# Roots of batch 0 on ScalarE and VectorE, another order of the first loads, and a new plan in an attention and gated-unit kernel

## The chip, the core and the metric

The kernel runs on one core of one Trainium2 chip. The core has TensorE (PE, matrix products; PEld is its weight load), VectorE (DVE), ScalarE (ACT), GpSimd (POOL) and SyncE (SP), which here only issues DMAs. The metric is the device time of one execution in microseconds (us). Groups in the profile give busy time in us and the mean of one instruction in nanoseconds (ns).

## The reference

Eight batches, eight heads, 576 tokens, 64 values in a head; all in float32. The weights come as float64 and are narrowed on the chip.

```python
def _attn_ref(q, k, v, g_norm):
    kv = np.einsum('bhsd,bhse->bhde', k, v)
    out = np.einsum('bhsd,bhde->bhse', q, kv)
    rms = np.sqrt(np.mean(out * out, axis=-1, keepdims=True) + 1e-06)
    return (out / rms * g_norm).astype(np.float32)

def _moe_ref(x, w_val, conv_w, w_out):        # x: (8, 576, 512), the heads side by side
    ...
    for k in range(K):                         # K = 5, causal
        gate_pre += conv_w[k][None, None, :] * xp[:, k:k + S, :]
    gate = 1.0 / (1.0 + np.exp(-gate_pre))
    val = x @ w_val
    return (gate * val @ w_out).astype(np.float32)
```

## The kernel before

Each batch goes through one chain. Two sums of products, k against v for each head (`kv_product`), give a 64x64 matrix a head; `kv_copy` moves them into a block-diagonal tile. `turn_q_rows` and `sort_q` transpose q of batches 0 and 1 on PE (later batches: `turn_q` on DVE). `raw_product` multiplies q by the matrices in five chunks of tokens: chunk 4 (64 tokens) first, then 3, 2, 1, 0 (128 each). For each chunk ACT squares (`square`, L499), DVE sums over a head (`sums`, L507), POOL raises the sum to the power -0.5 (`powers`, L513), and the result scales the chunk (`normalise`; on DVE at L528 for batches 0 to 2). The scaled chunk is transposed (`turn_x` on PE, `keep_x` on ACT for batches 0 and 1) into xT. From xT come the gate (`gate_start`, four `gate_tap`s on DVE, `gate_end`, a sigmoid on ACT) and the value product (`val_product` L590 for batches 0 and 1; later batches use a form with seven products instead of eight, `val_fast` L640). `gated` multiplies both, and an output product follows (`out_product` L671, or `fast_product` L735), then copy and store.

The weights, conv_w as one piece (cw), w_val and w_out as four pieces each, are loaded as pairs of 32-bit words by `stage_weight` into a ring of three buffers (w64) and narrowed to float32 in eight steps of `narrow_weight`: three on ACT, five on DVE. A w64 buffer is free again when step 6 is done. q of a batch is loaded as its last 64 tokens and two halves of the heads (`load_q_rows`, batches 0 and 1), k and v as two halves each (`load_half`), and their last 64 tokens as `load_tails`. All these loads are issued by SP, in order.

The order of all work is made when the program is built. Each step is given to a planner with its engine, an estimated time, a due time ("want"), what it needs and gives, the ring buffers it takes and frees, and for a DMA the time of its transfer ("load"). The planner runs a list schedule: of the steps that can start, it takes the one that can start first, and among equals the one with the smallest want. A table SHIFTS adds an offset to the wants of single steps, by the function's name and the batch (or the piece of weight). A step can't start earlier than its want less "ahead", which is 40 us, and 0 for loads. The list gives the order in which each engine gets its instructions; the engines themselves then wait on semaphores, not on planned times. While PE has nothing before 60 us of planned time, `keep_warm` (L397) fills the gap with products of the identity that are not used.

The wants of the loads at the start:

```python
    weight(("cw", 0), 0.0, 0.1, 0.1)
    ...
    loads_q(0, 0.01)
    loads_kv(0, 0.04)
    attention(0, 18.0, 1.8, 10.0, 5.0)
    for jt in range(NK):
        weight(("wval", jt), 0.09 + 0.01 * jt, 16.0 + 3.0 * jt, 0.5)
    ...
    loads_q(1, 0.14)
    loads_kv(1, 0.2)
    ...
        weight(("wout", jt), 0.3 + 0.01 * jt, begin + 1.0 + 4.6 * jt, 0.57)
```

Of the kernel before, what the change touches and what calls it, by code (L numbers as in the profile page):

```python
# [15 lines left out]
P = 128  # L16
# [5 lines left out]
    "fast_product": {1: 26, 2: 2, 3: 6},  # L22
    "gate_end": {7: 1.5},
    "gate_start": {4: 18.5},
    "gate_tap": {1: 38.5, 2: 38.5, 3: 74, 4: 70, 5: 49.5, 6: 86.5, 7: 45},
    "halo": {4: -0.5},
    "kv_product": {7: -5},
    "load_half": {("k", 3): -5.5, ("k", 4): -4, ("k", 5): 3.5, ("k", 7): -1.5, ("v", 0): -1.5,
        ("v", 4): -12, ("v", 5): -28.5, ("v", 6): -7.5, ("v", 7): -1.5},
    "load_q": {2: 23.5, 5: 17.5, 6: 8, 7: -9},  # L30
    "load_q_rows": {0: -173.5},
    "load_tails": {4: 11, 5: -2, 6: -21.5, 7: -18},
    "move_blocks": {7: 13},
    "normalise": {1: -26, 6: -27.5},
    "out_product": {0: 26},
    "powers": {3: -102, 4: 2, 7: -42.5},
    "raw_product": {2: -2, 4: -36, 6: -21.5, 7: 4.5},
    "square": {5: -170},
    "stage_weight": {("cw", 0): -313.5, ("wout", 1): -35.5, ("wval", 1): -123.5, ("wval", 2): -80.5,
        ("wval", 3): -85},  # L40
    "sums": {4: 2.5},
    "turn_blocks": {2: -1, 4: 48.5, 5: 32},
    "val_fast": {2: -5.5, 7: 18.5},
    "val_keep": {4: -120.5},
    "val_product": {0: 43, 1: 29},
    "weight_sums": {1: -14, 3: 19.5},
# [88 lines left out]
def kernel(  # L135
# [55 lines left out]
    FAST_VAL = range(2, B)  # L191
    FAST_OUT = range(2, B)
    ACT_NORM = range(3, B)
# [11 lines left out]
    def ps(kind, shape, name):  # L205
        return psum.tile(shape, FP32, tag=kind, bufs=BANKS[kind], name=name)
# [3 lines left out]
        "kv": 1, "kvbd": 2, "qT": 2, "tp": 1, "raw": 2, "mm": 4, "sq": 2, "ss": 3, "rt": 3,  # L210
# [188 lines left out]

    def kv_product(b, hp):  # L400
# [109 lines left out]
    def powers(b, c):  # L510
        n = heads(c)
        rt = work.tile([P, H], FP32, tag="rt", bufs=3, name=f"rt{b}_{c}")
        nc.gpsimd.tensor_tensor(  # L513
            out=rt[:, 0:n], in0=st["ss", b, c][:, 0:n], in1=mhalf[:, 0:n], op=ALU.pow)
        st["rt", b, c] = rt
# [252 lines left out]
    RATE = 0.27  # L768

# [6 lines left out]
    def attention(b, first, step, kv_first, turn_first):  # L776
# [40 lines left out]
        for n, c in enumerate(ORDER):  # L817
# [17 lines left out]
            )  # L835
            plan.add(
# [273 lines left out]
    for jt in range(NK):  # L1110
        weight(("wval", jt), 0.09 + 0.01 * jt, 16.0 + 3.0 * jt, 0.5)
# [70 lines left out]
```

## Time and profile before

| | us |
|---|---|
| median of 14 runs | 333.06 |
| lowest and highest | 332.35, 334.37 |
| the profiled execution, device time | 333.06 |
| its span, first to last instruction | 331.3 |
| busy: PE | 319.4 (96%) |
| busy: PEld, DVE | 245.4, 268.9 |
| busy: ACT, POOL | 185.8, 134.8 |
| DMA: moved, mean rate | 55.37 MB, 167 GB/s |

The span is what the profile's engines show; 1.76 us of the device time lie around it. A busy PE may be busy with filler, so its share alone doesn't say how much of it is needed. The windows in the prediction give, for stretches of the span, the busy time of PE, PEld, DVE, ACT and POOL (number of instructions in brackets), the granted PE clock as a share, and the share and rate of DMA. A line of the order of time gives start, duration, engine, line, operation, what it writes and reads, and in square brackets how long the engine was idle ahead of it and what released it. PEclk is full throughout: the mean granted clock is 0.997.

### The profile page before, as it was taken

What the parts mean: (1) busy time and instruction counts of PE and PEld (TensorE: products, weight loads), DVE (VectorE), ACT (ScalarE), POOL (GpSimd) and SP (SyncE); (2) the same over time, 40 slices, a digit from 0 to 9 for tenths busy, and PEclk for the clock granted to TensorE, in tenths of its full rate; (3) what the DMA queues carried; (4) which work ended last, traced back from release to release, by engine and by line L of the source; (5) the groups of instructions that cost most, each with busy time, mean ns of one, the idle gap of its engine ahead of it and who ended that gap; (6) DMA issues with size and microseconds to landing.
All of it is one profiled execution on the core that took longest, in us unless ns stands there. A gap on an engine that the chain in (4) does not pass through costs nothing.

```text
span 331.3 us, 6416 instructions
## 1 busy us (share of the span) xinstructions
PE 319.4 (96%) x2193; PEld 245.4 (74%) x2193; DVE 268.9 (81%) x479; ACT 185.8 (56%) x497; POOL 134.8 (41%) x178
## 2 busy tenths in 40 slices
PE   4999999999999999999999999999999999999993
PEld 4998877878755757587778758787885888888752
DVE  3168689799999729999999999999896697999601
ACT  3556965874366667675347848763676543534220
POOL 3006325203347969802558247777223274000000
PEclk9999999999999999999999999999999999999998
DMA  6999897697866886782966899465201235211233
GB/s 203 306 233 356 227 332 204 152 269 208 262 178 180 219 243 174 159 232 69 305 165 164 194 276 273 116 148 130 65 2 32 63 64 123 72 32 34 63 79 79
DMA packets 46014, 55.37 MB, mean 167 GB/s; under 512 B 15754, under 2 KB 36254, under 8 KB 45982
## 3 DMA queue, kind: packets, MB, share of 16 engines
q1 hardware_dynamic: 42558, 48.41, 53.1%
q0 software_dynamic: 3072, 6.30, 8.4%
q8 instruction: 17, 0.28, 0.4%
q10 hardware_dynamic: 352, 0.26, 0.4%
q14 instruction: 15, 0.12, 0.1%
HBM read 39.21 MB, written 9.44 MB: 147 GB/s over the span
## 4 chain that ended last, share of the span: by engine, by line
PE 81%; DVE 8%; DMA 3%; ACT 2%; issue 2%; SPq 2%; POOL 1%; DVEq 0%; ACTq 0%; POOLq 0%
PE va L640 13%; PE a L735 10%; PE raw L485 10%; PE cb L735 9%; PE out L671 8%; PE val L590 8%; PE vc L640 6%; PE out L678 4%; PE kv L408 4%; DVE gate L578 4%; PE vb L640 3%; PE qTps L446 3%; DMA vl<-in_v_dram 2%; PE kv L397 2%; PE xTps L538 2%
## 5 line engine op out<-in xcount | busy, mean ns | idle before, releaser
L513 POOL TENSOR_TENSOR rt<-ss,mhalf 128x8 f32<-128x8 f32 (+1 forms) x40 | 67.6, 1696 | 113.3 <-DVE ss L507 113.2
L578 DVE SCALAR_TENSOR_TENSOR gate<-xT,cwT,gate 128x576 f32<-128x576 f32 x128 | 99.1, 812 | 0.1
L561 POOL DMA_DIRECT2D xT<-y x96 | 52.9, 557 | 20.8 <-PE vc L640 7.5
L524 ACT ACTIVATE x<-raw,rt 128x64 f32<-128x64 f32 x180 | 39.6, 342 | 7.6 <-POOL rt L513 7.6
L485 PEld LDWEIGHTS raw<-kvbd,qT 128*128 128x128 f32 (+1 forms) x320 | 35.4, 180 | 8.4 <-issue 4.7
L485 PE MATMUL raw<-kvbd,qT 128*128 128x128 f32 (+1 forms) x320 | 39.1, 280 | 0.9 <-DVE x L528 0.6
L507 DVE TENSOR_REDUCE ss<-sq 128x8 f32<-128x520 f32 (+1 forms) x40 | 25.3, 633 | 10.2 <-ACT sq L499 9.7
L590 PE MATMUL val<-xT,wval 128*128 128x288 f32 x128 | 33.2, 409 | 0.0
L499 ACT ACTIVATE sq<-raw 128x512 f32<-128x512 f32 (+1 forms) x40 | 22.5, 562 | 18.5 <-PE raw L485 18.1
L671 PE MATMUL out<-wout,gv 128*128 128x512 f32 x64 | 28.5, 595 | 0.0
L590 PEld LDWEIGHTS val<-xT,wval 128*128 128x128 f32 x128 | 23.5, 190 | 5.8
L640 PE MATMUL va<-xs,vsum 128*128 128x288 f32 x96 | 27.3, 407 | 0.0
L603 DVE TENSOR_TENSOR gv<-gv,gate 128x576 f32<-128x576 f32 x32 | 23.6, 749 | 4.1 <-ACT gate L585 1.8
L585 ACT ACTIVATE gate<-gate 128x576 f32<-128x576 f32 x32 | 21.5, 690 | 8.9 <-DVE gate L578 8.8
L572 ACT ACTIVATE gate<-xT,cwT 128x576 f32<-128x576 f32 x32 | 24.1, 778 | 1.6 <-DVE gv L603 1.1
L735 PE MATMUL a<-wsum,sums 128*128 128x256 f32 x96 | 24.8, 381 | 0.0
L408 PEld LDWEIGHTS kv<-v,k 128*64 128x64 f32 x512 | 17.6, 137 | 5.6 <-issue 4.6
L671 PEld LDWEIGHTS out<-wout,gv 128*128 128x128 f32 x64 | 11.8, 190 | 13.2 <-issue 12.4
L640 PEld LDWEIGHTS va<-xs,vsum 128*128 128x128 f32 x96 | 18.0, 190 | 4.7
L744 DVE TENSOR_TENSOR ot<-cb,ot 128x256 f32<-128x256 f32 x24 | 10.0, 419 | 13.8 <-ACT ot L748 9.5
L408 PE MATMUL kv<-v,k 128*64 128x64 f32 x512 | 20.6, 226 | 0.2 <-DMA vl<-in_v_dram 0.2
L553 DVE STREAM_TRANSPOSE y<-x 128x512 f32<-128x512 f32 x24 | 16.8, 702 | 4.2 <-ACT x L524 4.2
(109 smaller groups left out, 563.8 us busy)
## 6 DMA issues: line engine op xcount, KB each, us to landing
q<-in_q_dram SPq DMA_DIRECT2D x96, 140.0 KB, 4.1
out_dram<-ot SPq DMA_DIRECT2D x140, 64.0 KB, 1.7
v<-in_v_dram SPq DMA_DIRECT2D x16, 512.0 KB, 6.2
k<-in_k_dram SPq DMA_DIRECT2D x16, 512.0 KB, 7.0
xT<-y POOLq DMA_DIRECT2D x96, 64.0 KB, 2.7
q<-in_q_dram SPq DMA_DIRECT2D x4, 512.0 KB, 6.3
w_wval<-in_moe_w_val_dram SPq DMA_DIRECT2D x4, 512.0 KB, 7.5
w_wout<-in_moe_w_out_dram SPq DMA_DIRECT2D x4, 512.0 KB, 6.6
```

What stands on the lines that cost most here:

```text
L408: nc.tensor.matmul(kvp[r * D:(r + 1) * D, hp, :], st["k", b, half][:, h, j, :] if j < NJ else kl[:, 2 * hp + r, :], st["v", b, half][:, h, ...
L485: nc.tensor.matmul(raw[row * m:(row + 1) * m, col * P:(col + 1) * P], st["qT", b][:, hp, c * P:c * P + m], kv_bd[b % 2][:, hp, :], start=T ...
L507: nc.vector.reduce_sum(out=ss[:, 0:n], in_=st["sq", b, c][:, 0:n], axis=AX.X)
L513: nc.gpsimd.tensor_tensor(out=rt[:, 0:n], in0=st["ss", b, c][:, 0:n], in1=mhalf[:, 0:n], op=ALU.pow)
L524: nc.scalar.activation(out=x[:, cols], in_=st["raw", b, c][:, cols], func=AF.Copy, scale=st["rt", b, c][:, h:h + 1])
L561: nc.gpsimd.dma_start(out=xTs[b % 2][i * TB:(i + 1) * TB, :, first:first + P], in_=y[a * TB:(a + 1) * TB, i])
L572: nc.scalar.activation(out=gate[:], in_=xTs[b % 2][:, jt, HALO:SX], func=AF.Copy, scale=cwT[:, K - 1, jt:jt + 1])
L578: nc.vector.scalar_tensor_tensor(out=gate[:], in0=xTs[b % 2][:, jt, tap * TB:tap * TB + S], scalar=cwT[:, tap, jt:jt + 1], in1=gate[:], op ...
L590: nc.tensor.matmul(val[:], wval[:, kc, jt * P:(jt + 1) * P], xTs[b % 2][:, kc, HALO + n * SV:HALO + (n + 1) * SV], start=(kc == 0), stop=( ...
L640: nc.tensor.matmul(st[bank, "val", b, mj][:], weights_[:, k], tokens()[:, k], start=(n in (0, 1, 3) and k == 0), stop=(k == NK // 2 - 1), ...
L671: nc.tensor.matmul(po[:], gv[:, jt, first:first + P], wout[:, jt, :], start=(jt == 0), stop=(jt == NK - 1),)
L735: nc.tensor.matmul(st[bank, i, p], tokens()[:, k], weights_[:, k], start=(n < 2 and k == 0), stop=(k == NK // 2 - 1), skip_group_check=True)
```

## The change

`powers` gets a second form for the chunks in `ROOTED`: ACT takes the square root (a new step, `root`, with a ring of its own), and DVE makes the reciprocal root of it in four small operations, the last three a Newton step. Chunks 3, 1 and 0 of batch 0 use it; chunks 4 and 2 of batch 0 and all other batches stay on POOL. A function `warm_up` issues 32 small products on PE at the start. The planner's rates and wants for the first loads and for batch 0's attention differ, its estimate of a power on POOL is 1.7 for 1.82, and the table SHIFTS is another one throughout.

```diff
 SHIFTS = {
-    "gate_tap": {1: 38.5, 2: 38.5, 3: 74, 4: 70, 5: 49.5, 6: 86.5, 7: 45},
-    "load_q_rows": {0: -173.5},
-    "stage_weight": {("cw", 0): -313.5, ("wout", 1): -35.5, ("wval", 1): -123.5, ("wval", 2): -80.5,
-        ("wval", 3): -85},
-    "val_product": {0: 43, 1: 29},
...
+    "gate_tap": {1: 46.5, 2: 6.5, 3: 56, 4: 67, 5: 82, 6: 82, 7: 27.5},
+    "load_half": {("k", 4): -26.5, ("k", 5): -25.5, ("k", 6): -12, ("v", 0): 2.5, ("v", 1): 5.5,
+        ("v", 2): 19, ("v", 3): 9.5, ("v", 4): -4, ("v", 5): -8.5, ("v", 6): -8.5, ("v", 7): -2.5},
+    "narrow_weight": {("wout", 0): 1.5, ("wout", 1): 3, ("wout", 2): -1.5, ("wval", 2): -15.5,
+        ("wval", 3): -47},
+    "stage_weight": {("wout", 0): -106.5, ("wout", 3): 66.5, ("wval", 0): -45},
+    "val_product": {1: 21.5},
...
+    ROOTED = {(0, NJ - 1), (0, 1), (0, 0)}
...
+    def warm_up():
+        banks = [ps("raw", [P, C], f"warm{n}") for n in range(2)]
+        for m in range(C // D):
+            for n in range(2):
+                for u in range(2):
+                    rows, to = (slice(r * D, (r + 1) * D) for r in (u ^ n, u))
+                    nc.tensor.matmul(
+                        banks[n][to, m * D:(m + 1) * D], ident[rows, 0:D], ident[rows, D:P],
+                        start=True, stop=True)
...
     def powers(b, c):
         n = heads(c)
-        rt = work.tile([P, H], FP32, tag="rt", bufs=3, name=f"rt{b}_{c}")
-        nc.gpsimd.tensor_tensor(
-            out=rt[:, 0:n], in0=st["ss", b, c][:, 0:n], in1=mhalf[:, 0:n], op=ALU.pow)
-        st["rt", b, c] = rt
+        st["rt", b, c] = rt = work.tile([P, H], FP32, tag="rt", bufs=3, name=f"rt{b}_{c}")
+        ss, rt = st["ss", b, c][:, 0:n], rt[:, 0:n]
+        if (b, c) not in ROOTED:
+            nc.gpsimd.tensor_tensor(out=rt, in0=ss, in1=mhalf[:, 0:n], op=ALU.pow)
+            return
+
+        t = st["root", b, c][:, 0:n]
+        nc.vector.reciprocal(rt, t)
+        nc.vector.tensor_tensor(out=t, in0=ss, in1=rt, op=ALU.mult)
+        for r, op, one in ((-0.5, ALU.mult, t), (1.5, ALU.add, rt)):
+            nc.vector.scalar_tensor_tensor(out=one, in0=t, scalar=r, in1=rt, op0=op, op1=ALU.mult)
+
+    def root(b, c):
+        n = heads(c)
+        st["root", b, c] = t = work.tile([P, H], FP32, tag="root", bufs=2, name=f"root{b}_{c}")
+        nc.scalar.activation(out=t[:, 0:n], in_=st["ss", b, c][:, 0:n], func=AF.Sqrt)
...
     RATE = 0.27
+    OPEN = 0.34
...
-                    takes=[(f"{name}{i}", b)], load=0.52 / RATE, ahead=0.0,
+                    takes=[(f"{name}{i}", b)], load=0.52 / (OPEN if b < 2 else RATE), ahead=0.0,
...
-                    load=(0.52 if i < 2 else 0.2) / RATE, ahead=0.0,
+                    load=0.52 / OPEN if i < 2 else 0.8, ahead=0.0,
...
-            load=0.52 * small / RATE, ahead=0.0,
+            load=0.52 * small / OPEN, ahead=0.0,
...
-    attention(0, 18.0, 1.8, 10.0, 5.0)
+    attention(0, 10.0, 1.0, 4.0, 2.0)
     for jt in range(NK):
-        weight(("wval", jt), 0.09 + 0.01 * jt, 16.0 + 3.0 * jt, 0.5)
+        weight(("wval", jt), 0.09 + 0.01 * jt, 20.0 + 4.0 * jt, 0.5)
...
         set_up()
+        warm_up()
```

## The prediction

> **What bounds the kernel now.** I read the windows of busy time first, then the groups of TensorE (PE) in the head, then PE's and SP's order of time there, last the roots on GpSimd (POOL).
>
> Windows (core us, then each engine's busy us):
> ```profile
> 0.00:22.90 22.90, 18.73 (x199) 17.60 (x199) 9.33 (x35) 10.39 (x26) 2.68 (x10) 1.00 0.96 248
> 22.90:39.75 16.85, 16.40 (x237) 14.77 (x237) 11.67 (x20) 13.35 (x33) 8.41 (x9) 1.00 0.99 292
> 39.75:60.00 20.25, 19.70 (x206) 15.87 (x206) 18.85 (x30) 12.57 (x25) 7.67 (x8) 1.00 0.77 239
> 60.00:100.00 40.00, 40.00 (x262) 28.97 (x257) 37.39 (x69) 23.03 (x48) 12.56 (x9) 1.00 0.82 222
> 100.00:140.00 40.00, 40.00 (x240) 24.79 (x239) 32.01 (x53) 26.90 (x82) 33.22 (x47) 1.00 0.76 197
> 140.00:220.00 80.00, 78.75 (x533) 61.31 (x533) 76.89 (x138) 50.61 (x161) 40.31 (x54) 1.00 0.74 196
> 220.00:300.00 80.00, 79.94 (x419) 63.36 (x418) 69.57 (x115) 42.20 (x111) 29.93 (x44) 1.00 0.29 70
> 300.00:331.30 31.30, 25.89 (x113) 18.77 (x111) 13.19 (x24) 6.75 (x16) 0.00 (x0) 0.97 0.23 59
> ```
> The first busy figure is PE's, the third VectorE's (DVE). From 39.75 (first value product) to 300, PE is idle 0.55 + 0 + 0 + 1.25 + 0.06 = 1.86 us; in the end stage 5.41. PE bounds everything after the head, with DVE close behind it (96% in 140 to 220). The head looks full too, but is not:
> ```profile
> L397 PE MATMUL kv<-ident 128*128 128x128 f32 x96 | 14.7, 310 | 0.2 <-ACT kvbd L418 0.2
> L446 PE MATMUL qTps<-ident,q 128*64 128x128 f32 (+1 forms) x160 | 10.4, 290 | 4.2 <-DMA q<-in_q_dram 4.2
> ```
> L397 is filler that computes nothing. Not work, of the span: filler 14.7, idle in the head 4.62, idle later 1.86 + 5.41, together 26.6 us. The rest, 304.7, the change doesn't touch. Where the head waits:
> ```profile
> 14.42 5.18 PE L397 MATMUL kv<-ident 128*128 128x128 f32 x44
> ...
> 20.84 2.05 PE L397 MATMUL kv<-ident 128*128 128x128 f32 x16
> 23.07 0.69 PE L408 MATMUL kv<-v,k 128*64 128x64 f32 x16 [0.17 <-DMA vl<-in_v_dram]
> ```
> ```profile
> 3.17 1.06 SPq L310 DMA_DIRECT2D w_wval<-in_moe_w_val_dram  x2
> ...
> 11.45 1.33 SPq L310 DMA_DIRECT2D w_wval<-in_moe_w_val_dram  x1
> 12.82 1.42 SPq L259 DMA_DIRECT2D k<-in_k_dram  x1
> ```
> Three value weights are issued ahead of the last half of k. That half, issued at 12.82 with landings of 8.8 to 10.1 us for k, is there at about 22.9; the second half of the k-v product starts at 23.07. (The release is put down to a later tail; by these landings k fits.) After it the roots go one by one on POOL:
> ```profile
> 28.89 6.43 POOL L513 TENSOR_TENSOR rt<-ss,mhalf 128x8 f32<-128x8 f32 x4 [0.45 <-DVE ss L507]
> ```
>
> **What the Trainium skill says.** "DMA: Bandwidth & Descriptors", Why small descriptors are slow (HBM only): each packet has a fixed cost, so 256-byte ones lose. The trace agrees: while tails pass (256 B rows), 3 us moved 0.63 MB (15 to 18 us) against 1.06 MB (9 to 12). "ScalarE: Activation LUTs", What ACT_TABLE_LOAD costs: 1283 ns for a load; the trace's two loads take 1283. Its section Table sets puts sqrt and sigmoid in different sets and cheap functions in every set; "ScalarE activation tables: per-element evaluation and per-set limits", Table sets in the compiler and the runtime, says loads are placed for the longest run. So the load at the start can be the sqrt set and the second, before the first sigmoid (47.63 us), stays: no load is added. No trace here shows a Sqrt. "TensorE: Matmul & The Clock Gate", What's actually happening: PE is slow until it has worked for some microseconds. Here 16 small transposes take 1.12 us at 4.16 and 0.68 at 24.38.
>
> **The change, part by part.** SP's order is read from the wants: of the loads that can start, the planner takes the one with the smallest want plus shift, and the nine weight pieces share three w64 slots, each free again only when its piece is converted. Tried on the kernel before, wants of -313.5 (cw), -173.5 (q), -123.4 and -84.9 (wval 1, 3), then v (-1.46), k, give exactly the recorded order.
>
> *Loads.* After: wout 0 (0.3 - 106.5) and wval 0 (0.09 - 45) come first, then cw (0), q, k 0, tails, k 1 (0.04), v 0 and v 1 (0.04 + 2.5). The w64 ring is full, so wval 1 to 3 stand behind v. Bytes up to the last of k and v: before 0.02 + q 1.18 + 3 weights 1.57 + k, v 2.10 + tails 0.26 = 5.13 MB; after, with 2 weights, 4.61. So one weight is gained, not three. By before's pace, (5.13 - 0.06) / (22.9 - 3.0) = 0.255 MB/us, 0.52 MB is 2.0 us. The first 3 us moved only 0.06 MB behind small transfers; a 512 KB transfer in front can fill the start sooner: 0 to 0.8, I take 0.3. Last half at 20.7 instead of 23.07: -2.4. The two weights put q back by 1.05 MB, some 3 us (q's tail at about 7, the rest at 10); PE's transposes of q (4.6 us warm: 0.68 + 4 x 0.98) still fit before v 0 at about 19, so this is hidden by the wait for v, and would cost nothing until q is 4 us later still. The other loads of SP (wval 1 to 3, q, k, v of batch 1) follow; up to batch 1's last k and v both orders carry some 9.7 MB, so those land near 36 us as before, and batch 1's raw product (45.24, wanted near 41 then) doesn't wait.
>
> *Roots.* Removed: three POOL powers of 1.61 us (6.43 / 4). Added for each: a Sqrt of 128x8 on ScalarE (ACT), 0.19 by the skill's 186 ns + 0.833 ns an element, up to 0.28 with a pointer bias, plus 1.28 if a table load falls there; and four small DVE steps. Nearest rows: 128x1 at 0.13 to 0.15 us, 128x20 from PSUM at 0.24; "VectorE: DVE Perf Modes", The TRN2 errata, prices a tensor_tensor at (N + 151) / 0.96, 0.166 us. I take 0.16 each, 0.65 for four; bounds 0.5 to 0.9. DVE gains 3 x 0.65 = 1.95 us, POOL loses 4.8. The Sqrt waits for the sums: ACT's weight conversions (0.72 each) queue behind it, and for them DVE; the four steps wait for the Sqrt, and on DVE sums and normalisations queue behind. On the path: before, five sums and five x from 26.82 to 36.10 with POOL pacing. With roots DVE paces: 0.42 + 4 x 0.69 sums, 1.95, 0.41 + 4 x 0.69 x = 8.3 us, end at 35.1 on the same clock. That is -1.0 for the last x, if no conversion falls between; each piece of weight does 2.97 us of DVE (0.42 + 0.69 + 0.42 + 0.69 + 0.75), so it may also be +2.
>
> *Batch 0's chain first.* After 23.07 the head still holds 18 fillers, 2.9 us, and 0.45 idle: 3.3 us. In the new order batch 1's q transposes (3.9), k-v and turning fill it, if q of batch 1 (7.1 MB, about 28 us) is there: after k-v at 20.7 come 1.4 product, about 0.9 copy to the bank, 4.4 raw, 0.9 turning two chunks, which ends at 28.3. I leave 1.7 us of loss (0.9 copy, 0.8 waits for x): -1.6. Bounds -3 and +2.
>
> *Warm-up.* 32 small matmuls after the identity is ready at 1.3 us, before q: 1.4 to 2.2 us in idle time. It costs nothing, since PE is idle for 4.2 us there; were q to land before 3.5 us, it would hold q's transposes up by what is left of it, and even that lies inside the wait for v. It speeds work that waits for v anyway.
>
> *Replanned rest.* 1.86 us of PE idle after the head is all that a better order there could win; the end stage needs its drain (last product ends 326.34, then copy and store, 5 us). I take 0; bounds -1.5 and, by rival D, +8.
>
> Sum: -2.4 - 1.6 = -4.0, with the roots' -1.0 inside the 1.6 (without them the last turnings, at 37.89 and 38.87, keep their places). The work PE does before the first value product is then 1.4 us less (half of batch 1's k-v is later), which is not lost. The profiled execution took 333.06 around a span of 331.30; the median is 333.06 too. 333.06 - 4.0 = 329.0.
>
> **Rivals.**
> - *A, forecast, 0.55:* 329.0, own range 327 to 331.
> - *B, the loads don't do what they say, 0.12:* wout 0 and wval 0 in front take the gain, tails and batch 1's small rows slow the end of v, and it lands near 22.5. Left are 0.5 + 1.0: 331.5. For it: k's halves took 8.8 to 10.1 us from issue to landing here, and the slow small rows of the tails now pass with 1.57 MB of k and v still behind them. Against: the byte count.
> - *C, more, 0.05:* the start runs at 0.35 MB/us, v at 19, and half of the 1.86 goes: -4.1 - 2 - 0.9 = 326.
> - *S, nothing left, 0.08:* PE starts earlier, but batch 1's k and v or weights come no sooner, and the head's gain comes back as waits: within 0.2%.
> - *D, slower, 0.20:* DVE becomes the bound in 140 to 220. It is idle there 3.1 of 80 us, and 8 of 40 in the stage before. PE running 4 us ahead eats this; the new wants of gates, turnings and sums, once they push more than 4 + 3.1 us of DVE work beyond 140, make PE wait for x sums and gated products. At 11 us of such work the waits are 8: -4 + 8 = 337. For it: 96% busy. Against: the tap shifts sum to 402 before and 367.5 after, so gates aren't later on the whole; and DVE has 20.2 idle us before 60 to be used (60 - 9.33 - 11.67 - 18.85).
>
> **How the numbers follow.** Faster by over 0.2% (about what a measurement of this kernel can tell from no change): A, B, C, 0.72; within: 0.08; slower: D, 0.20. The range 326.0 to 336.0 holds A, B, S, most of C and somewhat less than half of D.
>
> **What would show it.** SP's first issue is wout; second half of k-v at 20 to 21.5; fillers at or under 11 us; two table loads; four root steps at 0.13 to 0.2 us; first value product near 33 to 36; PE idle after it under 2.5 us until the end stage. Wrong if k-v starts after 22.5, if a third table load stands in the chain, or if PE waits for DVE by more than 4 us in 100 to 300.

## The result, and the profile after

The changed kernel takes 337.35 us (median of 10 runs, 336.05 to 339.74) against 332.90 us before (median of 48); the ratio is 1.0138 with the interval [1.0119, 1.0156]. It is 4.4 us slower where the prediction said 4 us faster. The span of the profiled execution is 335.5 us (before 331.3). The ratios here and below are made from fast runs alone, so that one can lie under the ratio of the medians. The ten executions go with their granted clock: the two at a mean of 0.996 took 336.05 and 336.44 us, the two at 0.989 took 339.55 and 339.74; the profiled one has 0.992, and the kernel before was at 0.996 or more whenever it ran beside an experiment. So of the 4.4 us about 1 goes with the clock, and some 3.3 are lost without it (an estimate from these figures).

The same windows as before, of the changed kernel (core us, then busy us of PE, PEld, DVE, ACT, POOL, the clock, the DMA share and GB/s):
```profile
0.00:22.90 22.90, 14.03 (x221) 12.96 (x223) 8.39 (x34) 9.52 (x24) 2.61 (x10) 0.99 0.99 247
22.90:39.75 16.85, 16.85 (x258) 15.19 (x259) 8.56 (x24) 11.64 (x32) 3.66 (x6) 0.91 0.92 266
39.75:60.00 20.25, 19.36 (x101) 15.26 (x100) 18.76 (x32) 13.93 (x27) 6.33 (x3) 1.00 0.83 240
60.00:100.00 40.00, 37.09 (x328) 28.62 (x327) 38.85 (x71) 23.02 (x45) 18.97 (x16) 1.00 0.71 207
...
140.00:220.00 80.00, 78.77 (x523) 61.86 (x522) 74.19 (x131) 50.41 (x156) 43.68 (x57) 1.00 0.75 201
```
Two things differ. PE, which was busy 40.00 of 40 us between 60 and 100, is busy 37.09, and VectorE is at 38.85 of 40 there (37.39 before). And up to 22.9 us PE does 4.7 us less, and comes out of it at a lower clock (0.91 in the second row; it was 1.00).

PE's waits, by what ended them (us in total, times, longest), and the same groups of fillers:
```profile
PE qTps L465 <- DMA q<-in_q_dram: 5.3, 1, 5.3
PE xTps L569 <- DVE x L559: 2.6, 1, 2.6
PE kv L427 <- DMA q<-in_q_dram: 1.8, 1, 1.8
```
```profile
L405 PE MATMUL kv<-ident 128*128 128x128 f32 x42 | 7.0, 327 | 0.9 <-ACT kvbd L437 0.9
L415 PE MATMUL warm<-ident 64*64 64x64 f32 x64 | 2.0, 314 | 1.4 <-POOL ident masks.py:199 1.4
```
Fillers fell from 14.7 to 7.0 us (and 2.0 of warm-up), but idle time rose from 11.9 to 19.7 us, so nothing was won by having fewer of them.

Busy time hides where the loss is, because fillers count as busy and a matmul at half clock counts double. I therefore priced each useful matmul of PE (no filler, no warm-up) at its full-clock duration and compared how much of it the two kernels have done by the same time. Positive is ahead of the kernel before; the count is good to about 0.5 us.
```
by (us)        20    30    40    50    60    70    80   100   300
changed      -0.6  -1.3  +0.6  -0.7  +0.8  -1.0  -3.2  -3.3  -4.7
```
So: about 1 us behind when batch 0's chain begins, 2 us won in it, 4.0 lost between 60 and 80, another 1.5 up to 300.

**The head.** SP's issues in the order of time (start, duration, queue, line):
```profile
8.45 1.33 SPq L267 DMA_DIRECT2D k<-in_k_dram  x1
9.82 1.86 SPq L276 DMA_DIRECT2D kl<-in_k_dram  x1
11.73 1.17 SPq L276 DMA_DIRECT2D vl<-in_v_dram  x1
12.95 2.92 SPq L267 DMA_DIRECT2D v<-in_v_dram  x2
...
25.97 3.48 SPq L318 DMA_DIRECT2D w_wval<-in_moe_w_val_dram  x3
```
Batch 1's tails (9.82 and 11.73) pass ahead of v; value weights 1 to 3 come at 25.97, behind k and v of both batches. PE in the same stretch:
```profile
21.05 0.69 PE L427 MATMUL kv<-v,k 128*64 128x64 f32 x16 [1.85 <-DMA q<-in_q_dram]
...
22.78 1.12 PE L427 MATMUL kv<-v,k 128*64 128x64 f32 x16 [0.35 <-DMA v<-in_v_dram]
...
26.56 4.43 PE L504 MATMUL raw<-kvbd,qT 128*64 128x128 f32 x40
...
39.37 2.11 PE L621 MATMUL val<-xT,wval 128*128 128x288 f32 x8
```
In the kernel before, the raw product:
```profile
25.70 4.43 PE L485 MATMUL raw<-kvbd,qT 128*64 128x128 f32 x40
```
(The pause of 1.85 is put down to q. The product doesn't read q; the first half of v, which it reads, landed at 20.9.) The second half of k-v starts at 22.78 instead of 23.07; after two pauses it takes 1.12 us for what took 0.69, since the granted clock is at half from 22.6 to 26.1 us, and the raw product starts at 26.56, 0.9 us later than before. One execution says little here. The first loads stand in this order in eight of the profiled kernels, and in them the second half began between 22.31 and 24.89 us; in three with the order of before between 22.42 and 23.07. And the half clock is not in all of them: in two kernels of the experiments below with the same head (one with a value product moved at the wait, one with batch 1's chain put earlier) k-v ran at full clock, and the first value product began at 38.29 and 38.19 us, 1.5 us earlier than before (39.75). ScalarE meanwhile, in batch 0's chain:
```profile
29.23 0.60 ACT L518 ACTIVATE sq<-raw 128x512 f32<-128x512 f32 x1 [0.30 <-PE raw L504]
29.85 1.28 ACT L546 ACT_TABLE_LOAD   x1
31.14 0.21 ACT L546 ACTIVATE root<-ss 128x8 f32<-128x8 f32 x1
31.26 1.07 ACT L518 ACTIVATE sq<-raw 128x512 f32<-128x512 f32 x2
```
A third table load stands before the first root, and the squares of the two last chunks stand behind it.

**60 to 80 us.** The wait of 2.6 us is one turning, of batch 1's last chunk:
```profile
68.44 0.66 PE L504 MATMUL raw<-kvbd,qT 128*64 128x128 f32 x8
71.69 0.63 PE L569 MATMUL xTps<-ident,x 128*128 128x128 f32 x4 [2.59 <-DVE x L559]
```
In the kernel before, the same chunk:
```profile
58.04 1.16 PE L485 MATMUL raw<-kvbd,qT 128*128 128x128 f32 x8
...
62.78 4.05 PE L590 MATMUL val<-xT,wval 128*128 128x288 f32 x16
66.66 0.60 PE L538 MATMUL xTps<-ident,x 128*128 128x128 f32 x4
67.10 9.87 PE L590 MATMUL val<-xT,wval 128*128 128x288 f32 x40
```
The chunk's raw product started at 63.46 (before at 58.04, and its turning at 66.66 without a wait). The raw products of batch 1 begin earlier than before (43.7 against 45.24), but chunk 2 stands behind four value products of batch 0 and chunk 1 behind three more. By 60 us all value products of batch 0 are used up, and the order puts only one of batch 1's ahead of this turning.

The plan itself has this wait. By the planner's own times, which are there when the program is built, PE is free at 62.67 and the turning starts at 65.98, 3.3 us later; the plan of the kernel before has no wait there. The new plan pays for it with a shorter head: its first value product stands at 34.21 us, against 40.16 in the plan of the kernel before, and the whole ends at 332.0 against 335.6. On the chip the wait came (2.6 us), and the shorter head didn't (39.37 against 39.75).

### The profile page after: what moved, and what is told of

Read it like the earlier page. It is cut to its first block, busy times and chain, and to the rows that moved or that the text cites. A ratio compares the mean times of both kernels' runs of the same rounds, so it can differ in the third digit from the quotient of the medians.

```text
span 335.5 us, 6442 instructions
## 1 busy us (share of the span) xinstructions
PE 315.8 (94%) x2203; PEld 240.6 (72%) x2203; DVE 269.8 (80%) x491; ACT 186.9 (56%) x501; POOL 136.9 (41%) x175
## 4 chain that ended last, share of the span: by engine, by line
PE 62%; DVE 13%; DMA 9%; ACT 5%; issue 3%; SPq 3%; POOL 3%; DVEq 0%; ACTq 0%; POOLq 0%
PE va L671 10%; PE out L702 8%; PE a L766 8%; PE cb L766 8%; PE val L621 7%; PE raw L504 6%; PE vc L671 5%; DMA q<-in_q_dram 4%; PE kv L427 4%; DVE gate L609 4%; PE out L709 3%; DMA v<-in_v_dram 3%; PE vb L671 3%; SPq L276 2%; POOL rt L534 2%
## 5 line engine op out<-in xcount | busy, mean ns | idle before, releaser
L534 POOL TENSOR_TENSOR rt<-ss,mhalf 128x8 f32<-128x8 f32 (+1 forms) x37 | 68.4, 1850 | 111.6 <-DVE ss L526 111.3
L427 PE MATMUL kv<-v,k 128*64 128x64 f32 x512 | 21.4, 231 | 2.2 <-DMA q<-in_q_dram 1.8
L427 PEld LDWEIGHTS kv<-v,k 128*64 128x64 f32 x512 | 18.6, 143 | 6.6 <-issue 4.2
L702 PEld LDWEIGHTS out<-wout,gv 128*128 128x128 f32 x64 | 11.9, 190 | 13.5 <-issue 13.2
L766 PEld LDWEIGHTS a<-wsum,sums 128*128 128x128 f32 x96 | 17.8, 190 | 2.9 <-ACT ot L781 0.3
```

The costliest lines, as they stand in the source:

```text
L427: nc.tensor.matmul(kvp[r * D:(r + 1) * D, hp, :], st["k", b, half][:, h, j, :] if j < NJ else kl[:, 2 * hp + r, :], st["v", b, half][:, h, ...
L534: nc.gpsimd.tensor_tensor(out=rt, in0=ss, in1=mhalf[:, 0:n], op=ALU.pow)
L702: nc.tensor.matmul(po[:], gv[:, jt, first:first + P], wout[:, jt, :], start=(jt == 0), stop=(jt == NK - 1),)
L766: nc.tensor.matmul(st[bank, i, p], tokens()[:, k], weights_[:, k], start=(n < 2 and k == 0), stop=(k == NK // 2 - 1), skip_group_check=True)
```

## The experiments

Each ratio is against the kernel before, run in turn with it on the same chip. "Ahead" and "behind" are useful PE work as in the table above.

**Parts of the change in its own order.** Only the named step differs from the changed kernel. Value weights without their conversion (and the same in the kernel before, as the yardstick):
```diff
     def narrow(key, dst, n):
+        if key[0] == "wval" and key[1] > 0:
+            if n == 6:
+                w = staged[key]
+                nc.vector.tensor_copy(
+                    dst, w[:, :, 1].rearrange("p (m c) -> p m c", m=dst.shape[1]))
+            return
```


> The changed kernel with its order of work untouched; pieces 1 to 3 of w_val are not converted but copied once as raw words (0.42 us of VectorE in place of 2.97, nothing on ScalarE), so the values are left out of the computation. Theory 1 (the late conversions of the value weights fill VectorE from 36 to 52 us and push batch 1's chain back, so TensorE waits at 68 to 73): the 2.6 us wait goes to under 0.7 and the time falls from 337.4 to 333 to 334.5. Theory 2 (it is TensorE's new order, all value products of batch 0 ahead of batch 1's chain): the wait stays over 2 us, the time falls by under 1 us.

> The same omission in the kernel before, pieces 1 to 3 of w_val copied and not converted, order untouched. Theory 1: here these conversions lie in idle VectorE time of the first 30 us, so nothing but noise: 332.5 to 333.2. If any VectorE or ScalarE work that is left out makes the kernel faster by itself: 2 us or more faster, and theory 1 gets no support from the other run.

Measured: 338.48 us, ratio 1.0101 [1.0038, 1.0165], and 332.77, 0.9999 [0.9982, 1.0016]. The first time says little, since its four executions lie between 334.32 and 339.79 us; the trace says more. The wait of 2.6 us at the turning is unchanged, although VectorE has only 10.6 us of work from 39.75 to 60 instead of 18.8. The freed time lies idle: its queue waits for the gate's first step on ScalarE, which comes 3.8 us after the first value product (4.1 in the changed kernel). Late conversions alone don't make this wait.

The roots back on GpSimd:
```diff
-        if (b, c) not in ROOTED:
+        if True:
             nc.gpsimd.tensor_tensor(out=rt, in0=ss, in1=mhalf[:, 0:n], op=ALU.pow)
             return
```


> The changed kernel with its order untouched, all roots back on GpSimd (no Sqrt, so no third table load). Theory 3 (the table load of 1.28 us and the root steps cost as much as GpSimd's queue saved): within 0.6 us of 337.4. Rival (the roots are worth having): GpSimd's powers stand one behind another again, the last x of batch 0 comes 1 to 2 us later, 338 to 339. Rival (the table load is what slowed it): 335.5 to 336.5.

Measured: 337.19 us, 1.0136 [1.0115, 1.0157]; the changed kernel has 1.0138. At the end these runs show no difference. In the head they show one: without the roots PE waits 1.3 us for x, and from the start of batch 0's raw product to the first value product it is 14.29 us; with them 12.81 (14.05 in the kernel before). That the 1.5 us aren't seen at the end may lie with the clock: this execution had no half clock in the head (its raw product began at 24.95) and one behind the wait of 2.6 us.

v of batch 0 moved ahead of batch 1's tails on SP:
```diff
+        vs = [f for f in found if f[1]["fn"] is load_half and f[1]["args"][0] == "v" and f[1]["args"][2] == 0]
+        found = [f for f in found if f not in vs]
+        at = next(n for n, f in enumerate(found) if f[1]["fn"] is load_tails and f[1]["args"][0] == 1)
+        found[at:at] = vs
```


> The changed kernel with one thing moved on SyncE's queue: v of batch 0 is issued ahead of batch 1's tails. Theory 4 (my count failed since these tails, 0.26 MB in rows of 256 B, pass before v): the second half of the k-v product starts at 20.7 to 21.5 and not at 22.8; the head ends 1 to 2 us earlier. If the wait at 68 to 73 comes from VectorE alone, the gain is eaten there and the time stays within 1 us of 337.4; if the head decides, 335.5 to 336.4.

Measured: 336.42 us, 1.0106 [1.0080, 1.0131]. PE in this run:
```profile
19.86 0.69 PE L427 MATMUL kv<-v,k 128*64 128x64 f32 x16 [0.45 <-DMA v<-in_v_dram]
...
21.82 0.69 PE L427 MATMUL kv<-v,k 128*64 128x64 f32 x16 [0.58 <-DMA v<-in_v_dram]
```
Both halves come about 1 us earlier and at full clock. This is the load order that the prediction assumed, and it gives 21.82, not 20.7. In the three other kernels below with v first it came at 21.75, 21.93 and 20.96; so all four lie under the eight with the tails first (22.31 to 24.89). This run is 2.2 us ahead at 40 us and about 3 behind at 80; the wait of 2.6 us is still there.

**Single steps at the wait.** A value product of batch 1 put ahead of the late turning, and, in another kernel, the sums of chunks (1,1) and (1,0) put right behind their squares (and x(1,0) two steps earlier, not shown):
```diff
+        move(pick(val_product, 1, 1, 1), pick(turn_x, 1, 0))
+        move(pick(keep_val, 1, 1, 1), pick(keep_x, 1, 0))
```
```diff
+        for c in (1, 0):
+            move(pick(sums, 1, c), pick(square, 1, c), 1)
```


> The changed kernel with its order untouched but for one product: TensorE does the value product of batch 1, piece 1, second half (1.94 us; it needs only chunks 4 to 2) ahead of the turning of chunk 0 and not behind it. Theory 2 (the new order leaves TensorE nothing to do while batch 1's last chunk is scaled): the wait at 69 to 72 falls from 2.6 to 0.6 to 0.9 us and the time by 1.5 to 3 us, to 334.5 to 336. Rival (the wait is only where a lag from the head comes out, so it turns up elsewhere): another wait of about 2 us within 10 us of it, time within 0.7 of 337.3.

> The changed kernel with its order untouched but for VectorE's queue in batch 1: the sums of chunks 1 and 0 stand directly behind their squares, and the scaling of chunk 0 two steps earlier, ahead of two steps of the output weights and of gate taps. Theory 5 (chunk 0's own chain is late since its steps queue on VectorE behind other work: its square ends at 65.3 and its sum starts at 67.6): chunk 0's x starts at 68.5 to 69.5 and not at 70.9, the wait falls to under 1.2 us, time 335 to 336.3. Rival (GpSimd's power sets it): x no earlier than 70, no gain.

Measured: 336.44 us, 1.0103 [1.0060, 1.0146], and 337.14, 1.0117 [1.0081, 1.0153]. In the first the wait splits into 0.45, 0.61 and 1.03 us within the next products; its time lies between the two forecasts. In the second x(1,0) starts at 70.28 instead of 70.86 and the turning waits 0.71, but then the value product waits 2.25 us for the copy of that turned chunk: on ScalarE it stands behind a gate's last step, which waits for a tap on VectorE. One step moved is one wait moved.

**The loads replanned.** The output weight's early want taken away and everything planned anew:
```diff
-    "stage_weight": {("wout", 0): -106.5, ("wout", 3): 66.5, ("wval", 0): -45},
+    "stage_weight": {("wout", 3): 66.5, ("wval", 0): -45},
```


> The changed kernel, planned anew with one shift taken out: piece 0 of w_out isn't due first. Then w64's oldest buffer is free early, and the other three value weights are issued between 9 and 18 us and not at 26 to 29. If the late value weights mattered, 334 to 335.5; after the run with the conversions left out I rather expect that they don't: 336 to 338, with VectorE less than 17 us busy from 40 to 60. A new plan moves everything a little, so under 1 us says nothing.

Measured: 350.87 us, 1.0528 [1.0471, 1.0585]. The value weights do load early again, so the three slots of w64 are what holds them back in the changed kernel: a slot comes free in the order in which it was taken, and the first is the output weight's, converted after 17 us. But the new plan loses 5 us at 90 to 100 and 11 more after 180. By its planner's own times this plan ends at 348.3 us, where the changed kernel's ends at 332.0; so this loss, too, stood in the plan before any run. A plan made from one different want moves the time by 13 us: three times what the whole change cost.

**Batch 1's chain put earlier.** In the first try its sums, powers and normalising stand ahead of taps and conversions on all engines, and raw products (1,1) and (1,0) earlier on PE; then with v first as well, and in a third kernel, with v in its old place, without the conversions of value weights 1 to 3:
```diff
+        put(pick(gate_tap, 0, 2, 1), (powers, 1, 3), (normalise, 1, 3))
+        put(pick(val_product, 0, 2, 0), (turn_x, 1, 3), (raw_product, 1, 1))
...
+        put(pick(kv_product, 2, 0), (turn_x, 1, 2), (raw_product, 1, 0), (val_product, 0, 3, 0))
```


> The changed kernel's loads, roots and fillers; only the steps of batch 1's chain (sums, powers, normalise, squares, turnings and raw products of chunks 3, 2, 1, 0) stand earlier on all four engines, ahead of gate taps and value products of batch 0. Theory (place in the queues): the loss of the changed kernel between 60 and 80 us comes from the steps of this chain standing late in in-order queues, while all value products of batch 0 are used up before. Then the wait of 2.6 us for the normalised chunk (1,0) falls under 0.5, no other PE wait over 1 us comes in its place up to 80 us, useful PE work at 80 us is 0 to 1.5 us behind the kernel before instead of 3.2, and the time is 334 to 335.5. Rival (DVE is simply full from 60 to 100 us): what is put ahead pushes taps and conversions back, a wait for DVE or for what follows it comes again within 30 us, work at 100 us is still 3 or more behind, and the time is 336.5 to 338.

> As the one with the chain put earlier, and v of batch 0 ahead of batch 1's k and v tails on SP as well. If both parts add (2.6 for the chain, 1 for the load): 333 to 334.5, about the kernel before. If DVE is full from 60 to 100 us, the earlier start only waits there: 336 to 337.5.

> The changed kernel with both at once: value weight pieces 1 to 3 are only copied instead of converted (their values are left out; some 8 us of VectorE less between 40 and 60 us), and batch 1's chain stands earlier on all engines. Each alone moved nothing that shows. Theory (the loss of 3 to 4 us between 60 and 80 us is VectorE work that the changed load order pushed behind 40 us, met by a chain that stands behind it in the queues, so that only both together lift it): PE waits at chunk (1,0)'s turning and the value products behind it fall from 4 to under 1 us in sum, useful PE work at 80 us is 0 to 1 us behind the kernel before, time 333 to 335. Rival (something else than VectorE sets the pace of that chain, for instance the round trip over four engines itself): the waits stay over 2.5 us, work at 80 us is over 2 behind, time 336 to 338.

Measured: 336.47 us, 1.0114 [1.0088, 1.0140]; 336.21, 1.0119 [1.0076, 1.0163]; 336.59, 1.0141 [1.0106, 1.0176]. The one wait became three of 1.5, 1.2 and 1.2 us, the same in the third kernel, and the work at 80 us is 2 to 3 us behind in all. By their numbers the rivals hold, but the trace shows that the edit missed its aim: raw product (1,2) still started at 52.1 us, behind four value products, so the chain was not begun earlier. These three don't separate the theories.

Hence the chain spread between the value products, one chunk behind each, without and with v first, and last with the two places mended at which those waited:
```diff
+            "PE": val_(0, 0) + val_(1, 1) + one_(turn_x, 4) + one_(raw_product, 2) + val_(1, 0) + one_(turn_x, 3)
+                + one_(raw_product, 1) + val_(2, 1) + one_(turn_x, 2) + one_(raw_product, 0) + val_(2, 0)
...
```


> The changed kernel with batch 1's chain spread between the value products of batch 0. The first try at this left raw product (1,2) behind four value products, so that chain still began its third chunk at 52 us; here raw product (1,2) comes behind two of them, (1,1) behind the third, (1,0) behind the fourth, with squares, sums, powers and normalising in step with it and gate taps, gate ends and q turnings behind. Theory (the loss between 60 and 80 us is the length of this chain, three rounds of square, sum, power and normalise over four engines, started too late, while VectorE is busy with work of the later value weights): turning (1,0) at 62 to 64 us instead of 71.7 without a wait, PE waits of 43 to 80 us under 1 us in sum, useful PE work at 80 us within 1 us of the kernel before, time 333 to 334.5. Rival (VectorE has no time left between 43 and 100 us, and what is put back is late in turn): the waits move to gates, q turnings or batch 2's chain, work at 100 us is 2.5 us or more behind, time 336 to 338.

> The same with v of batch 0 ahead of batch 1's k and v tails on SP, which alone put k-v 1 us earlier. If the chain was what ate that: 332 to 333.5, 1 us under the run without it. If VectorE has no time left: no difference over 0.5 us.

> As the last one with batch 1's chain spread between value products and v ahead of the tails, with the two places mended at which it waited (the key-value copy of batch 2 behind output weight conversions on ScalarE, 2.4 us; the copy of batch 1's turned chunk 0 behind that copy, 1.7 us), and with batch 2's first squares, sums and normalising ahead of the output weight conversions, three value products of batch 1 together. Theory (the loss between 60 and 80 us is an order in which one chain or another always reaches VectorE and ScalarE behind work that could wait, not a lack of engine time): no PE wait over 1.2 us between 43 and 85 us, useful PE work at 80 us at most 1 us behind the kernel before, time 332.5 to 334. Rival (VectorE has no time left: 58 of 60 us busy from 40 to 100): whatever stands behind is late in its turn, work at 100 us is 2.5 us or more behind, time 336 or more.

Measured: 340.86 us, 1.0237 [1.0184, 1.0289]; 338.59, 1.0179 [1.0134, 1.0225]; 342.08, 1.0283 [1.0257, 1.0310]. All are slower than the changed kernel. In the first two the turning of chunk (1,0) no longer waits (it starts at 65.61 in the second), but PE waits 2.4 us for the copy of batch 2's k-v and 1.3 and 1.7 us for the copy of the turned chunk, and the work at 100 us is over 4 us behind: the waits moved, as the rival said, and the times lie above both forecasts. The 2.3 us between the two can't be read as what v first gains, for the trace of the first has 10.2 us of half clock before the end and that of the second none. The last tells most. Two windows of it, and PE's next wait:
```profile
60.00:80.00 20.00, 20.00 (x175) 16.19 (x175) 16.41 (x32) 11.46 (x22) 6.76 (x8) 1.00 0.77 206
80.00:100.00 20.00, 13.20 (x124) 10.18 (x123) 19.52 (x36) 7.95 (x17) 5.53 (x5) 0.83 0.55 173
```
```profile
77.78 4.05 PE L621 MATMUL val<-xT,wval 128*128 128x288 f32 x16
88.62 2.08 PE L504 MATMUL raw<-kvbd,qT 128*128 128x128 f32 x8 [6.80 <-DVE x L559]
```
From 60 to 80 PE doesn't wait at all, with VectorE at 16.41 of 20, and at 80 us PE is 0.8 us ahead of the kernel before; the changed kernel was 3.2 behind. So in another order of the same steps the loss between 60 and 80 doesn't occur. At 81.8 the order written by hand ends and the planned one takes over: the sums of chunk (2,2) are done at 79.1, but its x comes at 87.89: it stands on VectorE behind the last steps of two output weights, three turnings of q, two gated products and a tap, and PE waits 6.8 us, with half clock from 85.3 to 92.2 us, which also slows what follows; at 100 us it is 7.9 behind. So the theory's forecast (no wait over 1.2 us up to 85, 332.5 to 334) failed, and the rival's numbers came (2.5 or more behind at 100 us, 336 or more). The order decides where PE waits; that VectorE has time enough for everything from 40 to 100 us is not shown by this kernel, which put VectorE's work off (19.52 of 20 us busy from 80 to 100). Against a mere lack of time stands the kernel without conversions, where VectorE idled and the wait stayed. Whether an order for the whole rest exists in which this comes out at 333 was not tried.

**The roots alone, in the kernel before.** The order, loads and fillers are those of before; three chunks take the new roots at the place of the power:
```diff
+        if (b, c) not in ROOTED:
+            nc.gpsimd.tensor_tensor(out=rt, in0=ss, in1=mhalf[:, 0:n], op=ALU.pow)
+            return
+        t = work.tile([P, H], FP32, tag="root", bufs=2, name=f"root{b}_{c}")[:, 0:n]
+        nc.scalar.activation(out=t, in_=ss, func=AF.Sqrt)
+        nc.vector.reciprocal(rt, t)
...
```


> The kernel before with nothing changed but the roots: chunks 3, 1 and 0 of batch 0 take ScalarE's square root and four VectorE instructions in the place of GpSimd's power; loads, order and fillers stay. By the prediction's term for the roots (1.0 us saved if no third table load falls into the chain, 0.3 lost if one does): 331.5 without a third load, 332.5 to 333.2 with it. What the changed kernel showed (a load of 1.28 us at the first root, no gain from the roots there) says the second. Rival: the roots on VectorE's queue behind weight conversions start late and cost 1 us or more: 334 or more.

Measured: 335.81 us, 1.0086 [1.0060, 1.0112]: 2.9 us slower, more than either side expected. ScalarE, then VectorE, in this run:
```profile
28.36 1.28 ACT L520 ACT_TABLE_LOAD   x1
29.66 0.21 ACT L520 ACTIVATE root<-ss 128x8 f32<-128x8 f32 x1
29.77 0.58 ACT L500 ACTIVATE sq<-raw 128x512 f32<-128x512 f32 x1
31.42 0.60 ACT L500 ACTIVATE sq<-raw 128x512 f32<-128x512 f32 x1 [1.07 <-DVE ss L508]
```
```profile
29.90 0.20 DVE L521 RECIPROCAL rt<-root 128x8 f32<-128x8 f32 x1 [1.39 <-ACT root L520]
30.14 0.17 DVE L522 TENSOR_TENSOR root<-ss,rt 128x8 f32<-128x8 f32 x1
...
32.16 0.68 DVE L537 TENSOR_TENSOR x<-raw,rt 128x512 f32<-128x512 f32 x1
```
The reader should follow one circle: the load delays the root; VectorE, which works in order, waits 1.39 us for it with the next sums behind; those sums hold a buffer that the next square on ScalarE needs (1.07 us). Later roots stand behind weight conversions and copies of q on ScalarE. Although this execution began its k-v 0.65 us earlier than before, x of the second chunk comes at 32.16 instead of 30.90 and the first value product at 41.20 instead of 39.75. From the raw product's start to there it is 16.13 us, against 14.05 before and 12.81 in the changed kernel: the same roots cost 2 us in the old order and save more than 1 in the new one.

**An earlier k-v, in the kernel before.** k and v of batch 0 ahead of the value weights on SP, with at most six fillers at a place and batch 1's small rows of q turned behind the raw product; then with batch 0's chain ahead of the weight conversions on ScalarE and VectorE (value weights 0 and 1 exchanged, output weight 1 loaded later), then that without the conversions of pieces 1 to 3, last with the output weight's conversion further back and the value weights in the order of their use:
```diff
+        kv = [f for f in found if f[1]["fn"] in (load_half, load_tails) and f[1]["args"][-1 if f[1]["fn"] is load_tails else 2] == 0]
+        found = [f for f in found if f not in kv]
+        at = next(n for n, f in enumerate(found) if f[1]["fn"] is stage_weight and f[1]["args"][0] == "wval")
+        found[at:at] = kv
```


> The kernel before with its order, but all of batch 0's k and v issued ahead of the value weights, at most 6 fillers in a gap, and batch 1's small q chunk turned behind batch 0's raw product. My forecast's step alone, without roots or a new plan. The second half of the k-v product at 17.5 to 19.5 (23.1 before), raw product at 20 to 21.5. If an earlier k-v is worth what it is earlier by: 328 to 329. If TensorE then waits for batch 1's q and k and v, whose bytes land when they did: 331.5 to 333.

> The kernel before with k and v of batch 0 ahead of the value weights, as in the run that failed on ScalarE's queue, but with the weight conversions behind the key-value copy, the squares, the sums and the normalising of batch 0 on ScalarE and VectorE, and wout 1 loaded behind k and v of batch 1. Roots stay on GpSimd. By the prediction's first term (an earlier end of k-v is worth its full amount): k-v's second half at 18.8 instead of 23.1, last turning of batch 0 at 35 to 36 instead of 38.9, first value product at 36 instead of 39.8, time 329 to 331. Rival (VectorE has little to spare between 40 and 100 us, so what the head gains is given back there): useful PE work 2 to 3 us ahead at 40 us and within 0.7 of the kernel before at 100 us, time 332.5 to 334.

> The same, with value weight pieces 1 to 3 only copied (their values are left out), which takes about 9 us from VectorE and 6.6 from ScalarE before 50 us. If VectorE is what gives the head's gain back: 329 to 331 here while the same order with conversions is 332.5 or more. If the gain reaches the end in both: no difference over 0.7 us between them. If both are 333 or more, the head's gain is lost to something else than VectorE.

> As b_kv_mend (the kernel before, k and v of batch 0 loaded ahead of the value weights, batch 0's chain ahead of the weight conversions), but the output weight's conversion on ScalarE, which made batch 1's key-value copy wait 8.4 us there, stands behind that copy and batch 1's first squares, and the value weights are loaded and converted in the order in which the products use them. The head is as in b_kv_mend: first value product at 36.2 instead of 39.8. If an earlier end of k-v is worth its amount at the end: 329 to 331. Rival (VectorE gives it back between 40 and 100 us): 2 to 3 us ahead at 40 us, within 0.7 at 100 us, 332.5 to 334.

Measured: 341.12 us, 1.0233 [1.0192, 1.0273]; 341.24, 1.0270 [1.0245, 1.0294]; 334.11, 1.0045 [1.0018, 1.0073]; 344.31, 1.0336 [1.0287, 1.0385]. In the first, k-v ends 4 us earlier, and then PE waits for the copy of it to the bank:
```profile
29.03 0.80 PE L397 MATMUL kv<-ident 128*128 128x128 f32 x2 [8.81 <-ACT kvbd L418]
29.76 7.20 PE L485 MATMUL raw<-kvbd,qT 128*64 128x128 f32 x40
```
That copy stood on ScalarE behind conversions of weights that now arrived later; and the raw product, 4.43 us at full clock, takes 7.20 after the pause. In the second the head is as expected (first value product forecast at 36):
```profile
18.23 0.69 PE L408 MATMUL kv<-v,k 128*64 128x64 f32 x16
...
36.19 2.11 PE L590 MATMUL val<-xT,wval 128*128 128x288 f32 x8
...
50.18 3.12 PE L485 MATMUL raw<-kvbd,qT 128*64 128x128 f32 x16 [8.44 <-ACT kvbd L418]
```
The first value product starts 3.6 us earlier than before, and useful work is 2.7 us ahead at 40 us. Then the same thing happens to batch 1's copy:
```profile
46.97 0.72 ACT L335 ACTIVATE wexp_wout<-wexp_wout,biases 128x512 uint32<-128x512 uint32 x1 [4.20 <-DVE wexp_wout L330]
```
An output weight's conversion, whose first step stood late on VectorE, blocks ScalarE for 4.2 us, with the copy behind it. Without conversions of the value weights the waits for the copies of batches 0 and 1 are 2.4 and 2.3 us, each with 3.4 us of half clock behind it, and the time is 334.11. In the last kernel batch 1's copy is on time, but batch 0's waits 2.7 us, and later PE waits 3.1 and 2.9 us for v and 3.9 for x. So the prediction's first term can be reached, but none of these kernels carried it to the end; each lost it again where a step queued behind a load or a conversion, and to the half clock behind these waits. No version here is faster than the kernel before.

## Why the prediction failed

**Loads, -2.4: failed, 0.3 came in the profiled execution.** The term put the last half at 20.7 us from 4.61 MB ahead of the end of k and v. Two steps of it were off. The order: batch 1's k and v tails have a smaller want than v of batch 0 and pass first, 0.26 MB that the byte count left out; moving v ahead of them gave 1.0 us, what 0.26 MB at 0.255 MB/us would. And the pace: with the assumed order the half came at 20.96 to 21.93 in four kernels, 0.3 to 1.2 us after the estimate, so the rate of the kernel before didn't quite hold for the shorter list. The 0.3 for a fuller start isn't seen in the end of the load. The 9.7 MB that the prediction counts up to batch 1's last k and v hold value weights 1 to 3 too; in the plan these wait for the oldest slot, and they come at 25.97, after batch 1's k and v. What a pause of PE costs was not in the sum at all: in the profiled execution PE paused for 1.85 and 0.35 us and ran k-v and the turning of batch 1's small rows at half clock, so that the raw product began 0.9 us later, not 2.4 earlier. In the four kernels with these loads whose head ran at full clock it began at 24.95 to 25.60, 0.1 to 0.8 us earlier than before. The prediction's own sign for this, k-v after 22.5, came true.

**Roots, -1.0: the table load was missed; in the head the gain came all the same.** The prediction concluded from the Trainium skill, "ScalarE activation tables: per-element evaluation and per-set limits", Table sets in the compiler and the runtime (loads placed for the longest run), that no load is added. The measurement decides: a third load, 1.28 us, stood before the first Sqrt, as the prediction named for the case. The sizes of the small steps were nearly right (0.20 and three times 0.17, sum 0.71 for 0.65; the Sqrt 0.21 to 0.24 for 0.19). Whether the whole pays depends on the order around it, since every root is a round trip to ScalarE on which VectorE's queue stops: in the old order the roots alone cost 2.9 us; in the new one the way from raw product to first value product is 1.5 us shorter with them than without, and at the end nothing of it can be told.

**Batch 0's chain first, -1.6: right.** From 30 to 60 us the changed kernel gains 2.1 us of useful work; with the powers back on GpSimd it gains 0.8 there, so the roots are part of it, as the prediction's sum had it.

**Warm-up, 0: not contradicted.** It is 2.0 us of busy time in the 8.7 us before q is there. No run leaves it out. That q comes later was hidden too, as said.

**Replanned rest, 0: failed, the largest term.** The reasoning was that 1.86 us of idle time is all that a better order can win, and so the term was taken at nothing. It can lose far more: 4.0 us went between 60 and 80, and 1.5 after. (Of these last, the waits explain little: PE is idle 1.7 us from 100 to 300, before 1.3. The rest is within twice the error of the count and stays open.) Rival D had the sign, the size and the engine (337, PE waiting for VectorE), the size by luck, for it had the wrong place: VectorE in 140 to 220 is less busy than before (74.19 against 76.89), and the sum of the tap shifts said nothing. What was late was batch 1's chain, one step of which stood behind value products on PE and another behind taps and conversions on VectorE. The last kernel with batch 1's chain spread out shows that in another order this stretch has no wait, and the plan shows that the new order had it from the start: 3.3 us by its own times, more than all the idle time from which the term was taken at nothing. The plan rests on a head 6 us shorter, for which it takes the loads to be faster than they were (the rate OPEN of 0.34; its own start for the first k-v is 17.42, and the chip's is 21.05). Whether a plan made with the chip's rate would be faster than the kernel before was not run.

The budget in useful work: -1.3 up to 30 us, +2.1 up to 60, -4.0 up to 80, -1.5 up to 300: 4.7 behind, and the span is 4.2 longer. Of the first term, 3.4 us at half clock are 1.7 us of work (an estimate), so without them the head would be about even at 30 us.

## What to carry to other kernels

A kernel that is full on its main engine and ordered by a plan has little to win from a new plan and much to lose: cost such a replan by following the next chain, step by step, through every queue it stands in, not by the idle time that is left; and read the waits in the plan itself, which here named the largest one before any run. A load that is moved later drags every instruction that waits for it, and all that queues behind those on an in-order engine: move the waiting instructions with it. When a change of several parts is predicted, price each round trip between engines by the queue that stops for it, not by the instructions alone.

## What the runs showed of the hardware

- A pause of PE can cost more than its length. In the 20 traces, before the last stores, the granted clock falls to half for 3.41, 6.83 or 10.24 us at a time. I cut each trace into windows of 3.41 us from the start of its clock record and took PE's idle share of the window ahead: with up to 0.50 idle, no window at full clock was followed by half clock; from 0.51 to 0.59, four of ten; from 0.65 on, all. So the same wait can cost nothing more, or 1.7 us more (half of 3.41, an estimate), by how it falls across the windows. After the waits of 8.8 and 8.4 us in the last group of experiments half clock lasted 10.24 us, in part still within the wait. Below, in columns as in the windows above, the head of the changed kernel, whose pauses fall into one window; its wait of 2.6 us, which falls across two; and the same wait with v first, in one.
```profile
19.20:22.60 3.40, 1.39 (x40) 1.28 (x40) 2.42 (x4) 0.69 (x1) 0.00 (x0) 1.00 1.13 300
22.60:26.00 3.40, 3.22 (x56) 3.13 (x56) 0.00 (x0) 0.73 (x2) 0.00 (x0) 0.51 1.02 330
67.00:70.40 3.40, 2.10 (x17) 1.43 (x15) 3.40 (x6) 2.87 (x6) 1.98 (x1) 1.00 1.00 261
70.40:73.80 3.40, 1.79 (x13) 1.64 (x14) 3.40 (x8) 1.50 (x3) 0.10 (x1) 1.00 0.96 239
```
```profile
67.40:70.80 3.40, 0.81 (x12) 0.60 (x9) 3.40 (x6) 1.16 (x3) 1.79 (x1) 1.00 1.08 271
70.80:74.20 3.40, 3.40 (x14) 2.97 (x13) 3.40 (x8) 1.77 (x3) 1.49 (x1) 0.50 0.85 218
```

- The Sqrt brought a table load of its own, 1.28 us, both times in the first root, though only cheap functions stood between it and the load at the start. The squares and copies after it needed none.
- GpSimd's power of 128x4 took 1.04 us at 27.40 in the kernel before, and 2.05 us at 47.33 in the changed one, where VectorE worked without a pause. Times on GpSimd are rough in these profiles, and that the one is the cause of the other was not tested.
